# Ranks behind the scores, lists cleared in larger pieces, and another order of loads and stores in a fused attention and two-layer expert kernel

## Chip, cores and metric

One NeuronCore of a Trainium2 chip. The metric is device microseconds of the whole program on that core; 707.65 us is the median of three runs of the kernel before.

## What is computed

The reference runs a linear attention with a decaying state over 4 batches, 8 heads, 768 steps and head width 48, and feeds its output through two expert layers (8 experts, 3072 tokens, width 384, inner width 1024):

```python
for t in range(S):
    state = f[:, :, t, :, None] * state + einsum('bhd,bhe->bhde', k[:, :, t], v[:, :, t])
    y[:, :, t] = einsum('bhd,bhde->bhe', q[:, :, t], state)
x = y as (3072, 384)
# each layer: every token goes to the expert with the largest logit
expert = argmax(x @ w_gate, axis=1); gate = softmax(x @ w_gate)[expert]
out[i] = gate[i] * (relu(x[i] @ w1[expert[i]]) @ w2[expert[i]])   # f = sigmoid(f_logit)
```

The first layer keeps only the first `capacity` tokens of an expert; a token's place is its rank among the tokens of its expert.

## The kernel before

The attention works on 24 tiles of 128 tokens (`NTILE`), six per batch. `_attention` (L303) is one software pipeline: in step `it` every stage of the table `STAGES` (L217) runs in the order of the table on tile `it - lag`; the first six steps use the same table with `gates` later. All engines' programs are written in that order, so the table is the order of each engine's queue. The loop runs over 28 steps, and a tail (L620 on) with its own hand-written order finishes the last tiles and starts the first expert group.

Per tile and with their lags: `load_x` (0) loads F (the gate logits) and the two halves of X (keys and queries, transposed), `load_v` (4) loads V, all from SyncE, each into rotating buffers (3 F, 4 X, 4 V); `bound` (1, VectorE, DVE) clips F; `gates` (2, ScalarE, ACT); `sums` (3, TensorE, PE) makes the running sums G; `expand` (3, ACT); `factors` (3, DVE) makes KQ; `keys_t` (5, PE and a copy on ACT) transposes the keys; `scores` (5, PE); `masked` (5, DVE) reads the scores out of PSUM; `updates` and `states` (6) advance the state; `output_s`, `output_i` (7, PE) and `rows` (7, ACT) give the tile's rows; `rows_t`, `rows_c` (8) and `logits` (9) the router's logits. PSUM is shared: kp, G, xp and the warm-up spins rotate through the two buffers of tag "tr"; the scores `sc` and the updates `kv` have the one buffer of tag "sc".

Routing goes by groups of three tiles (`RG`). `g_copy`, `g_turn` and `g_choose` (10) put six small DVE operations (`st.choice`, L96 to L126, the last the one-hot `oha`; with it ACT's exponential `exa`) into the list `small`; `step()` calls strewn through `masked`, `factors`, `states` and `bound` issue them one by one. `g_rank` (11) flushes what is left and calls `place` (L128), five small PE matmuls that read the one-hots; `g_store` (11) lists the following operations, which turn ranks into slots. `g_list` (14, GpSimd) scatters token numbers into the list `tab1` in DRAM, `g_save` (14, SyncE) stores the group's rows (582 KB) to DRAM. In the table `g_rank` and `g_store` stand after `keys_t` and ahead of `sums`; `g_save` stands first. `lead` (12) runs once, for tile 11: a matmul and some DVE operations that mark the tokens of the first expert group.

`side(i)` (L1586) runs ahead of a step's stages: the two lists `tab1` and `tab2` in DRAM (491,520 bytes each) are cleared in steps 11 and 18 by `_clear` (L284) from an SBUF tile `env.fill` of 60 words per partition, and weight chunks (`raw`, 256 KB each) are fetched in some steps. `after(i)` splits weight chunks in the steps of `SPLITS` (L210): ACT copies, GpSimd subtracts.

The clear, as it is (n is 60, t is 16):

```python
    n = env.fill.shape[1]
    t = E * RC * TW // P // n
    eng.dma_start(out=tab.rearrange("(p t n) o -> p t (n o)", p=P, t=t), in_=env.fill.unsqueeze(1).to_broadcast([P, t, n]))
```

Of the kernel before, what the change touches and what calls it, by code (L numbers as in the profile page):

```python
# [9 lines left out]
F32 = mybir.dt.float32  # L10
F32R = mybir.dt.float32r
BF16 = mybir.dt.bfloat16
I32 = mybir.dt.int32
# [9 lines left out]
DM = H * D  # L23
E = 8
EP = 32
FF = 1024
P = 128
# [5 lines left out]
W = DM + 4  # L33
C_GATE = DM
C_TID = DM + 1
RC = 3840

TW = 4
BIG = 1048576.0
FIRST = 65536.0  # L40
FILL = 1 << 20
# [157 lines left out]
def _route(*args, **kw):  # L199
# [15 lines left out]


STAGES = (  # L217
    ("g_save", 14),
    ("load_v", 4),
    ("load_x", 0),  # L220
    ("g_copy", 10),
    ("gates", 2),
# [3 lines left out]
    ("bound", 1),  # L226
    ("warm", 0),
    ("keys_t", 5),
    ("g_rank", 11),
    ("g_store", 11),  # L230
    ("sums", 3),
    ("g_turn", 10),
    ("g_choose", 10),
# [1 line left out]
    ("expand", 3),  # L235
    ("output_i", 7),
    ("scores", 5),
    ("lead", 12),
    ("masked", 5),
    ("factors", 3),  # L240
    ("rows", 7),
    ("rows_c", 8),
    ("g_list", 14),
    ("logits", 9),
)

# [34 lines left out]
    tc.add_to_no_dep_group(key, ins)  # L281


def _clear(eng, env, tab):  # L284
    n = env.fill.shape[1]
    t = E * RC * TW // P // n
    eng.dma_start(
        out=tab.rearrange("(p t n) o -> p t (n o)", p=P, t=t), in_=env.fill.unsqueeze(1).to_broadcast([P, t, n])
    )


# [11 lines left out]
def _attention(tc, env, fn, kq, vn, x1, tab1, early, masks, first, side, after, first_group):  # L303


    nc = tc.nc
    with ExitStack() as ctx:
# [14 lines left out]
        pair = lambda t: t.rearrange("p (a e) -> p a e", a=NPAIR)  # L322
        tiles = {}
        grp = {}
        NVB = 4
        NXB = 4
        fbuf = [e1.tile([P, DM], F32, name=f"F{i}") for i in range(3)]
        xbuf = [e1.tile([P, 2, NPAIR, P], F32, name=f"X{i}") for i in range(NXB)]

        lbuf = [e1.tile([P, H, 64], F32, name=f"L{i}") for i in range(2)]  # L330
# [5 lines left out]
        for xb in xbuf[1:]:  # L336
            nc.gpsimd.memset(xb, 0.0)

        def load_x(i):
            t = tiles[i] = _Bag()  # L340
            t.F = fbuf[i % 3]
            t.X = xbuf[i % NXB]
            nc.sync.dma_start(out=t.F, in_=fn[i])
            if i < 2:
                masks(i)
            for h in range(2):
                nc.sync.dma_start(out=t.X[h * 64 : h * 64 + D], in_=kq[i, h])
# [211 lines left out]
        def flush():  # L559
            while small:  # L560
                step()
# [10 lines left out]
        def g_store(i):  # L572
            if i % RG == RG - 1:
                ro = tiles[i].ro
                for a, b in zip(ro.slots, ro.sums):
                    small.extend((a, b))
                small.extend(ro.sums[len(ro.slots) :])
# [27 lines left out]
        def spin(i, n):  # L605
# [3 lines left out]

        locals_ = {  # L610
            f.__name__: f
            for f in (load_x, load_v, bound, gates, sums, expand, factors, keys_t, scores, masked, updates, states,
                      output_s, output_i, rows, rows_t, rows_c, logits, g_copy, g_turn, g_choose, g_rank, g_store, g_save, g_list, warm, lead)
        }
        begin, turn, divide, product, parts = first_group(p_2, p_1)
        for it in range(NTILE + 4):
            side(it)
            for nm, lag in (STAGES if it >= NFIRST else FIRST_STAGES):
                if 0 <= it - lag < NTILE:
                    locals_[nm](it - lag)  # L620
                elif nm == "sums" and it - lag == NTILE:

                    spin(it, 1)
            after(it)
# [6 lines left out]
        updates(n - 1)  # L631
        states(n - 1)
        keys_t(n)
        flush()
        tiles[n - 6].ro.place()
        g_store(n - 6)
        rows_t(n - 3)
        rows_c(n - 3)
        output_i(n - 2)
        scores(n)  # L640
        masked(n)
        rows(n - 2)
        logits(n - 4)
# [62 lines left out]
def _attention_general(tc, env, f, k, q, v, x1, tab1):  # L706

    nc = tc.nc
    EG = 4
    EW = D // EG  # L710
    with ExitStack() as ctx:
        gp = ctx.enter_context(tc.tile_pool(name="g_in", bufs=1))
        gps = ctx.enter_context(tc.tile_pool(name="g_ps", bufs=1, space=PSUM))
        st = gp.tile([P, EW, D], F32, name="g_st")
        nc.vector.memset(st, 0.0)
        tm = gp.tile([P, EW, D], F32, name="g_tm")
        with tc.For_i(0, S, TSTEP) as t0:
            tl = {}
            for nm, src in (("f", f), ("k", k), ("q", q)):
                t = gp.tile([P, TSTEP, D], F32, name="g_" + nm, tag="g_" + nm)  # L720
                sv = src.rearrange("b h s d -> (b h) s d")[:, bass.ds(t0, TSTEP), :]
                for g in range(EG):
                    nc.sync.dma_start(out=t[g * 32 : (g + 1) * 32], in_=sv)
                tl[nm] = t
            vt = gp.tile([P, TSTEP, EW], F32, name="g_v", tag="g_v")
            for g in range(EG):
                sv = v.rearrange("b h s d -> (b h) s d")[:, bass.ds(t0, TSTEP), g * EW : (g + 1) * EW]
                nc.sync.dma_start(out=vt[g * 32 : (g + 1) * 32], in_=sv)
            ft = tl["f"]
            nc.scalar.activation(ft, ft, AF.Exp, scale=-1.0)  # L730
            nc.vector.tensor_scalar(out=ft, in0=ft, scalar1=1.0, scalar2=None, op0=ALU.add)
            nc.vector.reciprocal(out=ft, in_=ft)
            yt = gp.tile([P, TSTEP, EW], F32, name="g_y", tag="g_y")
            sh = [P, EW, D]
            for t in range(TSTEP):
                ob = lambda a: a[:, t : t + 1, :].to_broadcast(sh)
                nc.vector.tensor_tensor(out=st, in0=st, in1=ob(ft), op=ALU.mult)
                nc.vector.tensor_tensor(
                    out=tm, in0=ob(tl["k"]), in1=vt[:, t, :].unsqueeze(2).to_broadcast(sh), op=ALU.mult
                )  # L740
                nc.vector.tensor_tensor(out=st, in0=st, in1=tm, op=ALU.add)
                nc.vector.tensor_tensor(out=tm, in0=st, in1=ob(tl["q"]), op=ALU.mult)
                nc.vector.tensor_reduce(out=yt[:, t, :], in_=tm, axis=AX.X, op=ALU.add)
            for g in range(EG):
                for b in range(B):
                    dst = x1.rearrange("(b s) w -> b s w", b=B)[b, bass.ds(t0, TSTEP), 0:DM]
                    dst = dst.rearrange("s (h e) -> h s e", h=H)[:, :, g * EW : (g + 1) * EW]
                    nc.sync.dma_start(out=dst, in_=yt[g * 32 + b * H : g * 32 + (b + 1) * H])
        nc.vector.memset(env.cum1, 0.0)
        _clear(nc.gpsimd, env, tab1)  # L750
        tid = gp.tile([P, TW], I32, name="g_tid")
        nc.gpsimd.iota(tid, pattern=[[0, TW]], base=0, channel_multiplier=1)
        with tc.For_i(0, NT, P) as r0:
            xr = gp.tile([P, W], F32, name="g_xr", tag="g_xr")
            nc.sync.dma_start(out=xr[:, 0:DM], in_=x1[bass.ds(r0, P), 0:DM])
            nc.vector.memset(xr[:, DM:W], 0.0)
            xp = gps.tile([P, NCC, P], F32, name="g_xp", tag="g_xp")
            for cc in range(NCC):
                nc.tensor.transpose(xp[:, cc], xr[:, cc * P : (cc + 1) * P], env.ident)
            xT = gp.tile([P, NCC, P], F32, name="g_xT", tag="g_xT")  # L760
            nc.vector.tensor_copy(out=xT, in_=xp)
            rt = gps.tile([P, 64], F32, name="g_rt", tag="g_rt")
            for cc in range(NCC):
                nc.tensor.matmul(rt[:, 0:E], xT[:, cc], env.wg1[:, cc, 0:E], start=(cc == 0), stop=(cc == NCC - 1))
            su = _route(
                nc, env, rt[:, 32 : 32 + E].unsqueeze(1), rt[:, 0:E].unsqueeze(1), 1, P, env.cum1,
                xr[:, C_GATE : C_GATE + 1], "ag", lim=env.lim,
            )
            nc.sync.dma_start(out=x1[bass.ds(r0, P), DM:W], in_=xr[:, DM:W])
            _scatter1(tc, "tab1g", tab1, su, tid, E * RC - 1)  # L770
            nc.vector.tensor_scalar(out=tid, in0=tid, scalar1=float(P), scalar2=None, op0=ALU.add)
# [699 lines left out]
def tile_attention_moe_moe(  # L1471
# [5 lines left out]
    nc = tc.nc  # L1477
# [84 lines left out]
    with ExitStack() as mo:  # L1562
# [9 lines left out]
            tc.tile_pool(name=nm, bufs=b, side="right", reuse_waits="tile")  # L1572
        )
        env.xr = R("xr", 2, mo)
        early = ExitStack()
        sel0 = cs[:, C_SEL : C_SEL + E]

# [8 lines left out]
        def side(i):  # L1586
            if i == 5:
                load_small()
            if i == 11:
                _clear(nc.sync, env, tab1)  # L1590
            if i == 18:
                _clear(nc.sync, env, tab2)
            if i == 8:
                late_setup()
            if i in (7, 12, 16, 20, 21, 22):

                wts.ahead = (7, 12, 16, 20, 21, 22).index(i) + 1
                wts.fetch()
            if i == SNAP + 14:
                M.take(g0)  # L1600
            if i == SNAP + 15:
                M.index(g0)
            if i == NTILE + 4:
                for j in range(g0.J):
                    M.gather(g0, j)
# [52 lines left out]
    with tc.If(fl > 0), ExitStack() as mo:  # L1658
# [19 lines left out]
        with tc.If(rd > 0):  # L1678
# [3 lines left out]
                nc.vector.tensor_copy(out=env.caps, in_=env.capn.to_broadcast([P, E]))  # L1682
                _attention_general(tc, env, f_nat, k_nat, q_nat, v_nat, x1, tab1)
            nc.vector.memset(env.cum2, 0.0)
            _clear(nc.gpsimd, env, tab2)
            for i in range(NTILE):
                nc.sync.dma_start(out=out[i * P : (i + 1) * P, :], in_=env.zrow[:, 0:DM])
            tb = yrp.tile([P, 2, NOVF], I32, name="o_tb")
# [97 lines left out]
```

## Time and profile before

| what | value |
|---|---|
| three runs | 705.44, 707.65, 709.28 us (median 707.65) |
| the profiled execution | 706.58 us, its span 704.8 us, mean granted clock 0.975 |
| PE busy | 663.6 us of the span (94%) |
| DVE, ACT, GpSimd busy | 400.8, 305.6, 211.9 us |
| DMA | 97.55 MB, mean 138 GB/s over the span |

Times inside the execution are microseconds from the span's start. PE is TensorE's matmuls; the clock column is the share of full speed (2.4 GHz) that TensorE was granted. A wait "<- issue" is idle time for which the profile shows no releaser. The queue q8 of the DMA views carries instructions, q1 SyncE's transfers and q0 GpSimd's.

### The profile page before, as it was taken

The numbers are of one execution on the slowest core, as the hardware profiler recorded it, in microseconds if no ns is written. First come the engines' busy times: TensorE is split into PE (matmuls) and PEld (weight loads), VectorE is DVE, ScalarE is ACT, GpSimd is POOL, SyncE is SP. The second block draws the span as 40 slices with busy tenths as digits, with TensorE's granted clock in tenths as the row PEclk, the third lists the DMA queues.
The fourth block names the chain that finished last, engine by engine and source line by source line (L and its number), as shares of the span: only waits on it lengthen the run. The fifth ranks groups of instructions, "written<-read, shape, count | busy, mean of one in ns | idle before, by whom it ended". The sixth has DMA issues, their size and how long they took to land.

```text
span 704.8 us, 17652 instructions
## 1 busy us (share of the span) xinstructions
PE 663.6 (94%) x6867; PEld 615.6 (87%) x6867; DVE 400.8 (57%) x1067; ACT 305.6 (43%) x649; POOL 211.9 (30%) x232
## 2 busy tenths in 40 slices
PE   7889878888899999999999999999999999999995
PEld 4778767776799999999999999899998899999994
DVE  3644546554557657576566864557555455565642
ACT  4665546453345344344434443144334343354421
POOL 2122435246334114140422221234424132224211
PEclk9998999899999999999999999999999999999998
DMA  8885797412269344373737350177445354435300
GB/s 199 221 176 159 186 191 193 130 41 89 72 196 275 114 142 142 113 189 86 216 88 174 90 188 13 34 221 216 111 129 167 103 165 131 141 119 166 108 25 21
DMA packets 59439, 97.55 MB, mean 138 GB/s; under 512 B 15820, under 2 KB 29102, under 8 KB 59347
## 3 DMA queue, kind: packets, MB, share of 16 engines
q1 hardware_dynamic: 51667, 80.70, 41.7%
q0 software_dynamic: 7680, 15.64, 8.1%
q8 instruction: 56, 0.92, 0.6%
q14 instruction: 36, 0.29, 0.1%
HBM read 80.54 MB, written 16.60 MB: 138 GB/s over the span
## 4 chain that ended last, share of the span: by engine, by line
PE 86%; DMA 6%; DVE 3%; issue 3%; ACT 1%; POOL 0%; DVEq 0%; ACTq 0%; POOLq 0%
PE hpm L1142 29%; PE ypm L1166 10%; PE ypm L1168 10%; PE ypm L1167 10%; DMA out_dram<-yr,tdm 6%; PE G L374 4%; PE y L486 4%; PE tpm L1118 2%; PE sc L414 2%; PE y L476 2%; PE kv L439 2%; PE warm L608 2%; PE kp L403 2%; PE tym L904 2%; PE xp L510 1%
## 5 line engine op out<-in xcount | busy, mean ns | idle before, releaser
L1166 PE MATMUL ypm<-hhm,w1h 128*128 128x288 f32 (+11 forms) x456 | 153.6, 337 | 1.8 <-DVE hlm L1154 1.8
L1167 PE MATMUL ypm<-hlm,w1h 128*128 128x288 f32 (+11 forms) x456 | 150.1, 329 | 0.0
L1168 PE MATMUL ypm<-hhm,w1l 128*128 128x288 f32 (+11 forms) x456 | 150.1, 329 | 0.0
L1142 PE MATMUL hpm<-xhm,w0h 128*128 128x288 f32 (+11 forms) x432 | 147.2, 342 | 0.0
L1142 PE MATMUL hpm<-xhm,w0l 128*128 128x288 f32 (+11 forms) x432 | 143.0, 332 | 0.0
L1153 ACT ACTIVATE hhm<-hpm 128x288 fp32r<-128x288 f32 (+11 forms) x144 | 69.5, 483 | 168.1 <-PE hpm L1142 165.8
L1142 PE MATMUL hpm<-xlm,w0h 128*128 128x288 f32 (+11 forms) x432 | 137.5, 332 | 0.0
L1154 DVE SCALAR_TENSOR_TENSOR hlm<-hpm,hhm 128x288 fp32r<-128x288 f32 (+11 forms) x144 | 78.1, 542 | 101.5 <-ACT hhm L1153 101.3
L293 POOL DMA_INDIRECT xrm<-x,idcm x64 | 71.0, 1109 | 136.9 <-PE hpm L1142 57.3
L1166 PEld LDWEIGHTS ypm<-hhm,w1h 128*128 128x128 f32 x456 | 85.7, 188 | 4.3 <-DVE hlm L1154 1.9
L1168 PEld LDWEIGHTS ypm<-hhm,w1l 128*128 128x128 f32 x456 | 85.7, 188 | 2.0
L1167 PEld LDWEIGHTS ypm<-hlm,w1h 128*128 128x128 f32 x456 | 85.8, 188 | 1.7
L1142 PEld LDWEIGHTS hpm<-xhm,w0h 128*128 128x128 f32 x432 | 81.2, 188 | 2.2
L1142 PEld LDWEIGHTS hpm<-xhm,w0l 128*128 128x128 f32 x432 | 81.3, 188 | 1.7
L1142 PEld LDWEIGHTS hpm<-xlm,w0h 128*128 128x128 f32 x432 | 80.3, 188 | 1.9
L271 POOL DMA_INDIRECT tab<-pos,sum x30 | 33.5, 1118 | 141.4 <-DVE sum L181 135.0
L271 POOL DMA_INDIRECT out_dram<-yr,tdm x34 | 41.2, 1212 | 89.4 <-DVE yr L980 83.3
L1004 DVE TENSOR_TENSOR w0l<-raw,w0h 128x512 fp32r<-128x512 f32 x90 | 60.2, 686 | 9.3 <-ACT w0h L1003 8.9
L1004 DVE TENSOR_TENSOR w1l<-raw,w1h 128x512 fp32r<-128x512 f32 x90 | 59.7, 688 | 0.3
L1003 ACT CAST w0h<-raw 128x512 fp32r<-128x512 f32 x96 | 57.3, 617 | 1.0 <-DMA raw<-in_w_dram 1.0
L1003 ACT CAST w1h<-raw 128x512 fp32r<-128x512 f32 x96 | 56.9, 622 | 0.4 <-DMA raw<-in_w_dram 0.4
L421 DVE TENSOR_TENSOR SC<-sc,cs 128x512 f32<-128x512 f32 x24 | 16.6, 690 | 65.4 <-PE sc L414 65.4
(224 smaller groups left out, 914.6 us busy)
## 6 DMA issues: line engine op xcount, KB each, us to landing
raw<-in_w_dram SPq DMA_DIRECT2D x192, 256.0 KB
X<-in_kq_dram SPq DMA_DIRECT2D x48, 192.0 KB
x<-xr SPq DMA_DIRECT2D x8, 582.0 KB
F<-in_fn_dram SPq DMA_DIRECT2D x24, 192.0 KB
Vn<-in_vn_dram SPq DMA_DIRECT2D x24, 192.0 KB
xrm<-x,idcm POOLq DMA_INDIRECT x64, 4.6
tab<-fill SPq DMA_DIRECT2D x2, 480.0 KB
x<-yr SPq DMA_DIRECT2D x2, 388.0 KB
```

The lines of the kernel that those rows point to most:

```text
L271: ins = tc.nc.gpsimd.indirect_dma_start(out=dst, out_offset=bass.IndirectOffsetOnAxis(ap=idx, axis=0), in_=src, in_offset=None, bounds_che ...
L293: nc.gpsimd.indirect_dma_start(out=dst, out_offset=None, in_=src, in_offset=bass.IndirectOffsetOnAxis(ap=idx, axis=0), bounds_check=bound, ...
L374: nc.tensor.matmul(t.G[:, a], t.L[:, 2 * a : 2 * a + 2].rearrange("p h d -> p (h d)"), env.cs[:, C_INC : C_INC + P], start=True, stop=True,)
L486: nc.tensor.matmul(t.y[u, h, e], t.SC[u, h, a], t.Vn[u, v0 : v0 + D], start=False, stop=a == NPAIR - 1,)
L1003: nc.scalar.copy(out=hi, in_=raw)
L1004: eng.tensor_tensor(out=lo, in0=raw, in1=hi.bitcast(F32), op=ALU.subtract)
L1142: nc.tensor.matmul(hp[:, :N], w[:, c, fs], x[:, c, :N], start=(k == 0), stop=(k == len(parts) - 1))
L1153: nc.scalar.activation(hh[:, :N], hp[:, :N], AF.Relu)
L1154: nc.vector.scalar_tensor_tensor(out=hl[:, :N], in0=hp[:, :N], scalar=0.0, in1=hh[:, :N].bitcast(F32), op0=ALU.max, op1=ALU.subtract)
L1166: nc.tensor.matmul(g.yp[d][:, :N], w2h[:, fc, ds_], hh[:, :N], start=(fc == 0), stop=False)
L1167: nc.tensor.matmul(g.yp[d][:, :N], w2h[:, fc, ds_], hl[:, :N], start=False, stop=False)
L1168: nc.tensor.matmul(g.yp[d][:, :N], w2l[:, fc, ds_], hh[:, :N], start=False, stop=(fc == NFC - 1))
```

## The change

The table of stages: `load_f` is split from `load_x` and runs one step ahead (lag -1, four F buffers), `load_v` has lag 3 and five V buffers, and both stand first; `g_save` goes to the end of the table with lag 15; `g_rank` and `g_store` move behind `scores` and `lead`, and `lead` gets lag 13. In the tail the rank of the third-last group (tiles 15 to 17) goes behind `scores(n)`, and one spin stands where it was. The clears read a tile of 960 words per partition, one piece of 3840 bytes for each partition; it lies in a buffer of the pool of gathered rows and is filled by GpSimd at the start.

```diff
--- before.py
+++ after.py
@@ -215,8 +215,8 @@
 
 
 STAGES = (
-    ("g_save", 14),
-    ("load_v", 4),
+    ("load_f", -1),
+    ("load_v", 3),
     ("load_x", 0),
     ("g_copy", 10),
     ("gates", 2),
@@ -226,8 +226,6 @@
     ("bound", 1),
     ("warm", 0),
     ("keys_t", 5),
-    ("g_rank", 11),
-    ("g_store", 11),
     ("sums", 3),
     ("g_turn", 10),
     ("g_choose", 10),
@@ -235,12 +233,15 @@
     ("expand", 3),
     ("output_i", 7),
     ("scores", 5),
-    ("lead", 12),
+    ("lead", 13),
+    ("g_rank", 11),
+    ("g_store", 11),
     ("masked", 5),
     ("factors", 3),
     ("rows", 7),
     ("rows_c", 8),
     ("g_list", 14),
+    ("g_save", 15),
     ("logits", 9),
 )
 
@@ -281,11 +282,11 @@
     tc.add_to_no_dep_group(key, ins)
 
 
-def _clear(eng, env, tab):
-    n = env.fill.shape[1]
+def _clear(eng, fill, tab):
+    n = fill.shape[1]
     t = E * RC * TW // P // n
     eng.dma_start(
-        out=tab.rearrange("(p t n) o -> p t (n o)", p=P, t=t), in_=env.fill.unsqueeze(1).to_broadcast([P, t, n])
+        out=tab.rearrange("(p t n) o -> p t (n o)", p=P, t=t), in_=fill.unsqueeze(1).to_broadcast([P, t, n])
     )
 
 
@@ -322,9 +323,9 @@
         pair = lambda t: t.rearrange("p (a e) -> p a e", a=NPAIR)
         tiles = {}
         grp = {}
-        NVB = 4
+        NVB = 5
         NXB = 4
-        fbuf = [e1.tile([P, DM], F32, name=f"F{i}") for i in range(3)]
+        fbuf = [e1.tile([P, DM], F32, name=f"F{i}") for i in range(4)]
         xbuf = [e1.tile([P, 2, NPAIR, P], F32, name=f"X{i}") for i in range(NXB)]
 
         lbuf = [e1.tile([P, H, 64], F32, name=f"L{i}") for i in range(2)]
@@ -336,11 +337,14 @@
         for xb in xbuf[1:]:
             nc.gpsimd.memset(xb, 0.0)
 
+        def load_f(i):
+            t = tiles[i] = _Bag()
+            t.F = fbuf[i % 4]
+            nc.sync.dma_start(out=t.F, in_=fn[i])
+
         def load_x(i):
-            t = tiles[i] = _Bag()
-            t.F = fbuf[i % 3]
+            t = tiles[i]
             t.X = xbuf[i % NXB]
-            nc.sync.dma_start(out=t.F, in_=fn[i])
             if i < 2:
                 masks(i)
             for h in range(2):
@@ -609,10 +613,11 @@
...
         begin, turn, divide, product, parts = first_group(p_2, p_1)
+        load_f(0)
         for it in range(NTILE + 4):
...
@@ -631,13 +636,14 @@
         updates(n - 1)
         states(n - 1)
         keys_t(n)
-        flush()
-        tiles[n - 6].ro.place()
-        g_store(n - 6)
+        spin(n, 1)
         rows_t(n - 3)
         rows_c(n - 3)
         output_i(n - 2)
         scores(n)
+        flush()
+        tiles[n - 6].ro.place()
+        g_store(n - 6)
         masked(n)
         rows(n - 2)
         logits(n - 4)
...
@@ -1572,6 +1578,10 @@
             tc.tile_pool(name=nm, bufs=b, side="right", reuse_waits="tile")
         )
         env.xr = R("xr", 2, mo)
+
+        fill = env.xr.tile([P, 4, W], F32, name="xfill", tag="xr").rearrange("p j w -> p (j w)")
+        fill = fill.bitcast(I32)[:, 0 : E * RC * TW // P]
+        nc.gpsimd.memset(fill, FILL)
         early = ExitStack()
         sel0 = cs[:, C_SEL : C_SEL + E]
 
@@ -1587,9 +1597,9 @@
             if i == 5:
                 load_small()
             if i == 11:
-                _clear(nc.sync, env, tab1)
+                _clear(nc.sync, fill, tab1)
             if i == 18:
-                _clear(nc.sync, env, tab2)
+                _clear(nc.sync, fill, tab2)
             if i == 8:
                 late_setup()
             if i in (7, 12, 16, 20, 21, 22):
...
```

## Rows read from the trace of the kernel before

**Rows 1.** Page, the chain that ended last, share of the span by engine.

```profile
PE 86%; DMA 6%; DVE 3%; issue 3%; ACT 1%; POOL 0%; DVEq 0%; ACTq 0%; POOLq 0%
```

**Rows 2.** Windows by stage: length, busy us of each engine, clock, DMA share.

```profile
25.60:158.50 132.90, 112.73 (x2961) 99.95 (x2960) 70.67 (x196) 76.17 (x157) 45.30 (x68) 0.91 0.65 157
158.50:179.10 20.60, 16.27 (x410) 13.29 (x407) 9.91 (x47) 7.24 (x17) 11.68 (x13) 0.92 0.36 106
179.10:704.80 525.70, 514.66 (x3264) 489.73 (x3264) 308.30 (x805) 209.69 (x453) 149.68 (x134) 1.00 0.45 131
```

**Rows 3.** Timeline of PE: start, us, line (two sums; the last spin).

```profile
30.27 1.06 PE L374 MATMUL G<-cs,L 128*128 128x128 f32 x8
...
40.00 1.06 PE L374 MATMUL G<-cs,L 128*128 128x128 f32 x8
...
158.49 0.38 PE L608 MATMUL warm<-zrow,oneb 128*128 128x512 bf16 x1
```

**Rows 4.** Timeline of PE: a turn, breaks, rank waits (idle before, releaser).

```profile
43.43 0.46 PE L414 MATMUL sc<-KQ 64*64 64x64 f32 x16 [0.73 <-issue]
...
50.16 0.57 PE L414 MATMUL sc<-KQ 64*64 64x64 f32 x22 [1.67 <-issue]
...
73.84 0.41 PE L264 MATMUL rt<-cs,lts 96*128 96x96 f32 x3
...
80.94 0.17 PE L130 MATMUL rt<-oha,trib 128*128 128x24 bf16 x1 [2.57 <-DVE oha L120]
...
98.43 0.61 PE L486 MATMUL y<-Vn,SC 64*64 64x48 f32 x15 [3.37 <-issue]
...
109.43 0.55 PE L439 MATMUL kv<-Vn,KT 64*64 64x48 f32 x20 [0.61 <-issue]
...
138.43 0.68 PE L439 MATMUL kv<-Vn,KT 64*64 64x48 f32 x32 [3.23 <-issue]
...
166.38 0.17 PE L130 MATMUL rt<-oha,trib 128*128 128x24 bf16 x1 [3.19 <-DVE oha L120]
```

**Rows 5.** Waits of PE to 179.1 us: us in total, times, the longest.

```profile
PE rt L130 <- DVE oha L120: 13.3, 6, 3.2
```

**Rows 6.** DMA, all queues, from 90.4 to 94.9 us.

```profile
DMA packets 2020, 0.76 MB, mean 169 GB/s; under 512 B 1877, under 2 KB 1880, under 8 KB 2020
```

**Rows 7.** DMA, instruction queue, from 94.9 to 97 us: packets, MB, share.

```profile
q8 instruction: 1, 0.02, 5.1%
```

**Rows 8.** Windows of 10 us: busy by engine, granted clock, DMA share, GB/s.

```profile
80.00:90.00 10.00, 9.06 (x184) 8.19 (x186) 3.88 (x15) 4.77 (x10) 0.97 (x4) 0.83 0.69 180
120.00:130.00 10.00, 7.43 (x118) 6.38 (x118) 4.05 (x12) 3.96 (x9) 2.48 (x4) 0.66 0.67 181
```

**Rows 9.** Timeline of all engines around the rank of step 16.

```profile
76.35 0.69 DVE L421 TENSOR_TENSOR SC<-sc,cs 128x512 f32<-128x512 f32 x1 [2.15 <-PE sc L414]
...
77.71 0.66 PE L403 MATMUL kp<-cs,KQ 128*128 128x128 f32 x4
...
78.44 1.04 DVE L108 TENSOR_TENSOR dla<-lsa,mxa 128x24 f32<-128x24 f32 x1
...
79.64 0.57 ACT L405 COPY KT<-kp 128x512 f32<-128x512 f32 x1
```

**Rows 10.** Timeline of ACT in the tail: the copy of the last keys.

```profile
163.28 0.58 ACT L405 COPY KT<-kp 128x512 f32<-128x512 f32 x1 [1.32 <-PE kp L403]
```

**Rows 11.** DMA, all queues, from 76.5 to 82.4 us.

```profile
DMA packets 990, 1.55 MB, mean 262 GB/s; under 512 B 135, under 2 KB 699, under 8 KB 989
```

**Rows 12.** DMA, instruction queue, from 82.4 to 84 us.

```profile
q8 instruction: 1, 0.02, 4.0%
```

**Rows 13.** Timeline of PE: the first updates.

```profile
18.79 0.68 PE L439 MATMUL kv<-Vn,KT 64*64 64x48 f32 x32 [1.60 <-ACT L L365]
```

**Rows 14.** Timeline of GpSimd at the start: the X buffers cleared.

```profile
1.66 2.73 POOL L337 MEMSET X<- 128x1024 f32 x3
```

**Rows 15.** DMA, instruction queue, from 25.6 to 158.5 us.

```profile
q8 instruction: 24, 0.39, 1.3%
```

More of the change, by code (lines that the diff above doesn't have):

```diff
@@ L611, in _attention @@
             f.__name__: f
-            for f in (load_x, load_v, bound, gates, sums, expand, factors, keys_t, scores, masked, updates, states,
+            for f in (load_f, load_x, load_v, bound, gates, sums, expand, factors, keys_t, scores, masked, updates, states,
                       output_s, output_i, rows, rows_t, rows_c, logits, g_copy, g_turn, g_choose, g_rank, g_store, g_save, g_list, warm, lead)
@@ L749, in _attention_general @@
         nc.vector.memset(env.cum1, 0.0)
-        _clear(nc.gpsimd, env, tab1)
+        _clear(nc.gpsimd, env.fill, tab1)
         tid = gp.tile([P, TW], I32, name="g_tid")
@@ L1684, in tile_attention_moe_moe @@
             nc.vector.memset(env.cum2, 0.0)
-            _clear(nc.gpsimd, env, tab2)
+            _clear(nc.gpsimd, env.fill, tab2)
             for i in range(NTILE):
```

## The prediction

> **What bounds the kernel now.** I read the chain of waits first: 86% of it is TensorE (PE) [rows 1], so what moves the end is time in which PE stands or runs slowly. The windows by stage say where that is [rows 2]: the experts, from 179.1 us on, keep PE busy for 514.66 of 525.70 us at full clock, and no part of the change touches them. The attention loop from 25.6 to 158.5 us has PE busy for 112.73 of 132.90 us at a granted clock of 0.91. The whole case lies there and in its tail, to 179.1 us.
>
> How far is the loop from its own pace? Two undisturbed steps (a step is one tile) run from 30.27 to 40.00 us, 4.87 us each [rows 3]. From the sums at 40.00 to the spin that stands in for them at 158.49 are 17 steps: 118.5 us. At pace that would be 17 x 4.87 = 82.8 us, plus five turns of at most 0.41 us and five ranks of some 0.3 us (five matmuls of about 0.17 us, pipelined) [rows 4]: 86 us. **Some 32 us are lost.** The waits of PE and its timeline name them:
> - 13.3 us in six waits of the rank matmul (L130) for the one-hot on VectorE (DVE) [rows 5]; one is the 2.57 us at 80.94, the last the tail's 3.19 us at 166.38 [rows 4].
> - Four breaks of 0.73, 1.67, 3.37 and 0.61 us in the middle of a group of matmuls that waits for no operand [rows 4]. No instruction packet moves on the DMA engines from 90.4 to 94.9 us, one does right after [rows 6, 7], and PE, which stopped at 95.06, resumes at 98.43: I read these as PE's instruction fetch arriving late.
> - 3.23 us before the state updates at 138.43 [rows 4]: `updates` and `scores` share one PSUM tag, so it waits until `masked` has read the scores, and `lead`'s DVE operations stand ahead of `masked`.
> - Half clock (1.2 of 2.4 GHz): (1 - 0.91) x 132.9 = 12.0 us in the loop and (1 - 0.92) x 20.6 = 1.6 in the tail [rows 2]. A stretch of 10 us at 0.83 costs 1.7 us, one at 0.66 costs 3.4 [rows 8]. The 0.66 and three of about 0.83 follow rank waits (8.5 us), about 3.5 follow the breaks of 1.67 and 3.37, and the tail's follows its rank.
>
> **A. Ranks behind the scores.** The five small matmuls move; they issue no DMA, and DVE's order stays, since no DVE operation stands between the old place and the new. Around step 16 the DVE chain is masked at 76.35, then `dla` at 78.44, and the one-hot that lets the rank go at 80.94, 4.6 us after masked; PE had finished transposing the keys by 78.37 [rows 9, 4]. PE now first does sums, row transposes, outputs and scores, and reaches the new place 4.87 us after the last scores, which is 4.87 less 0.2 us after masked began: it just fits. In the four other loop ranks the chain takes 3.7 to 4.6 us. **The wait that comes next** is on ScalarE (ACT): its exponential for the rank waits for `dla`, which took 1.04 us beside GpSimd's weight split, and the copy of the transposed keys queues behind it, 79.64 to 80.21 [rows 9]. The row transposes take the PSUM buffer that this copy frees, and PE would be there after the sums, at 78.2 + 0.9 = 79.1: a new wait of 1.1 us. The same rows around the other four give 0.25, 0, 1.1 and 0. In the tail the key copy ends at 163.86 [rows 10] and the one-hot at 166.38; with a spin, transposes, outputs and scores in between (2.2 us) some 1.1 of the 3.19 us stay. Behind the rank PE has logits and the next step's outputs; behind its result DVE has the slots, in the order of before. A = -13.3 + 3.5 = **-9.8 us** (to -13.3 if DVE is quicker without GpSimd beside it; 0 if another wait takes all of it).
>
> **B. The clock after ranks.** 8.5 + 1.6 = 10.1 us are to be had. Clock fell after breaks of 1.67 us and more, not after 0.73, nor directly after the 3.23. New waits are 1.1 us or less, but `lead`'s stays and others may come. I take two thirds: **-6.5 us** (0 to -10.1).
>
> **C. Clears in 3840-byte pieces.** Each list of 480 KB goes out in 2048 pieces of 240 bytes now, after it in 128. From 90.4 to 94.9 us, 1877 of 2020 packets are under 512 bytes, and 0.76 MB move at 169 GB/s [rows 6]: at that rate of packets a clear needs nearly 5 us. At the 262 GB/s of a crowded stretch without a clear [rows 11] 480 KB need 1.9 us. So each gives back some 3 us of all 16 DMA engines. No fetch moved in the 4.5 us before 94.9, and PE ran out at 95.06; with 3 us less in the queue it does not. C = -(3.37 + 1.67) - 3.5 of clock = **-8.5 us** (0 to -8.5). What the page says against it: the Trainium skill, DMA: Bandwidth & Descriptors, Queues, rings and completion order, has each DMA engine serve its queues in turn, packet by packet, so that a fetch on its own queue would not wait behind another queue's backlog. By that C would be nil. Rows 6 and 7 speak for a wait behind the backlog but don't prove it; it is rival 2.
>
> **D. The cover that goes.** The rank waits have hidden late fetches too. Around step 16 none begins from 76.5 to 82.4 us, with a store, two X loads, V and F moving, and one does from 82.4 to 84 [rows 11, 12]; PE lost nothing because it stood for 2.57 us and then ran at half clock. Without that it would come to the end of its instructions some 3 us early. Step 22 repeats it. A store (582 KB a group) is issued one to two steps later and behind F, V and X, so it meets other fetches; of the loop's stores two fall among loads. I put **+5 us** (0 to +15, three breaks like that at 98.43 with 1.7 us of clock each).
>
> **E. Loads.** SyncE blocks on the same waits: F on the last step's gates, V on its outputs, X on its factors; each load queued behind them has a step or more before its use, and the store waits for gates long done. V a step earlier, with a fifth buffer, can shorten the 1.60 us before the first updates at 18.79 [rows 13], where V is queued behind four X; X queues behind one more F. **-1 us** (-2 to +1). GpSimd's added clear of 960 words costs about 0.9 us, by the 2.73 us of three X buffers of 1024 [rows 14]; it delays buffers that SyncE reaches later than that, so nothing, or 0.9 us if they are what is late.
>
> **F. `lead` one step later** flushes six choice operations ahead of itself, while PE is in outputs and scores; its own wait of 3.23 us moves along: 0 (-1 to +2).
>
> Sum: -9.8 - 6.5 - 8.5 + 5 - 1 = -20.8. The profiled execution took 706.58 us, within the runs' 705.44 to 709.28 and 1.07 under their median, so **686 us**.
>
> **Rivals.**
> 1. Fetches take the ranks' place. Loads, stores and weights must now pass in about 5 instead of 7 us a step, and the share of the DMA engines, 0.65 over the loop [rows 2], comes to 0.65 x 132.9 / 112 = 0.77. For it: the long fetch delay of step 16. Against: the regular steps of rows 3 had no break. D is then +15 and B half: 706.6 - 9.8 - 3 - 8.5 + 15 - 1 = 699 us.
> 2. The breaks are not the clears' work. For it: breaks of 0.73 and 0.61 us without a clear in the queue. C = 0, the rest as forecast: 694 us. Beside it stands the Trainium skill, Runtime: NRT & Kernel Launch, Instruction fetch mechanics: crossing an instruction block costs little and is mostly hidden.
> 3. Slower. Fetches come late at nearly every one of the loop's 24 blocks [rows 15], each break as at 98.43 (3.37 us and 1.7 of clock). From five such breaks on, 25 us, the gain of A, B, C and E (25.8) is eaten; eight give 706.6 - 25.8 + 8 x 5 = 721 us. Against: only four of the 24 are late now.
> 4. The order is changed but nothing is gained, since the key copy and the shared PSUM tag hold PE as long as the one-hot did: A and B nil, and D eats most of C: 703 to 707 us.
>
> **How the numbers follow.** Forecast 0.60, rival 1 0.18, rival 2 0.14, rival 3 0.04, rival 4 0.04. The range goes from all terms at their favourable ends (-13.3 - 10.1 - 8.5 - 1, about 674) to rival 1: 674 to 700. A measurement of this kernel tells some 0.5%, 3.5 us, from no change. Faster takes the forecast and rivals 1 and 2: 0.92; same rival 4: 0.04; slower rival 3: 0.04.
>
> **What would show it.** Right: rank matmuls without a DVE wait in the loop; row transposes that wait for ACT by about 1 us in two steps; no packets of 240 bytes and no break after the clears; a mean clock above 0.95 in the loop; sums starting every 4.9 to 5.2 us; experts unchanged at about 526 us. Wrong: new "issue" breaks behind stores or X loads, with the fetch late; the 3.37 us break still there at the second clear; a shift at the experts.

## The result, and the profile after

Four runs of the changed kernel took 688.11 to 691.49 us, median 689.44, against 707.81 for the kernel before in the same comparison: a ratio of 0.9746 with a 95% interval of 0.9709 to 0.9783. The forecast was 686 us with a range of 674 to 700 and 0.92 for faster. The profiled execution took 689.96 us, with a span of 688.1, 16.7 us less than the one of before.

The page, chain by engine and all DMA packets (before, the packets of the span were 59,439, of them 15,820 under 512 bytes: the 4096 pieces of 240 bytes are what went):

```profile
PE 87%; DMA 7%; DVE 2%; issue 2%; ACT 1%; POOL 0%; DVEq 0%; ACTq 0%; POOLq 0%
...
DMA packets 55599, 97.55 MB, mean 142 GB/s; under 512 B 11724, under 2 KB 25006, under 8 KB 55507
```

Windows by stage of the changed kernel, cut at the same events as [rows 2]: the sums of the step that began at 25.6 there, the spin in place of the sums, the first expert matmul (length; busy us of PE, PEld, DVE, ACT, GpSimd; clock, DMA share, GB/s):

```profile
24.80:144.30 119.50, 106.49 (x2961) 94.42 (x2960) 70.80 (x196) 75.41 (x157) 45.01 (x68) 0.96 0.66 174
144.30:161.50 17.20, 15.37 (x411) 12.28 (x408) 9.86 (x46) 7.10 (x17) 11.72 (x13) 1.00 0.45 131
161.50:688.10 526.60, 515.58 (x3264) 489.79 (x3264) 308.29 (x805) 209.94 (x453) 151.42 (x134) 0.99 0.45 131
```

The loop gave 13.4 us, the tail 3.4, the start 0.8; the experts took 0.9 more. With the same 2961 matmuls in the loop, PE stood idle for 119.50 - 106.49 = 13.01 us instead of 20.17 (7.2 less), and was busy for 106.49 instead of 112.73 (6.2 less): the second is the clock. The waits of PE in the loop and most of the tail name most of the 13 us (further breaks without an operand follow one by one below):

```profile
PE kv L443 <- issue: 3.5, 2, 2.7
PE kv L443 <- DVE SC L425: 2.4, 1, 2.4
PE xp L514 <- ACT KT L409: 2.0, 2, 1.0
...
PE rt L259 <- DVE skip L1591: 1.4, 1, 1.4
...
PE rt L130 <- DVE oha L120: 0.2, 1, 0.2
```

Against 13.3 us in six waits [rows 5], the ranks (L130) wait 0.2. In their place stand two waits of the row transposes for the key copy on ACT, and breaks without an operand ("issue"). In PE's timeline (start, length, operation, idle time before it):

```profile
61.03 0.45 PE L443 MATMUL kv<-Vn,KT 64*64 64x48 f32 x17 [0.77 <-issue]
74.11 0.55 PE L514 MATMUL xp<-cs,xr 128*128 128x128 f32 x3 [1.00 <-ACT KT L409]
76.88 0.46 PE L418 MATMUL sc<-KQ 64*64 64x64 f32 x15 [0.86 <-issue]
87.11 0.61 PE L490 MATMUL y<-Vn,SC 64*64 64x48 f32 x15 [0.60 <-issue]
92.11 0.82 PE L378 MATMUL G<-cs,L 128*128 128x128 f32 x5 [1.14 <-issue]
98.98 0.88 PE L443 MATMUL kv<-Vn,KT 64*64 64x48 f32 x20 [2.69 <-issue]
113.55 0.55 PE L514 MATMUL xp<-cs,xr 128*128 128x128 f32 x3 [1.00 <-ACT KT L409]
127.30 0.42 PE L259 MATMUL rt<-xT,wg1s 128*32 128x128 f32 x6 [1.36 <-DVE skip L1591]
130.70 0.57 PE L443 MATMUL kv<-Vn,KT 64*64 64x48 f32 x12 [2.37 <-DVE SC L425]
```

With two of 0.36 and 0.30 us (at 42.63 and 52.45) the breaks sum to 6.7 us in the loop, against 6.4 in [rows 4]. They are others, though: the 1.67 and 3.37 behind the clears are gone, 0.86, 1.14 and 2.69 are new. They are read as late instruction fetches: at the longest PE stopped at 96.29 us; no packet of q8 moves from 90.7 to 96.4, and one fetch does from 96.4 to 97.6 (DMA, instruction queue, in that window):

```profile
q8 instruction: 1, 0.02, 5.7%
```

In all seven breaks of the loop PE resumes 1.3 to 1.5 us after such a fetch has landed.

The last two lines of the timeline are the step of `lead`, which had one wait of 3.23 us [rows 4]. Behind it the clock falls:

```profile
130.00:136.00 6.00, 5.30 (x63) 4.88 (x65) 2.49 (x5) 1.67 (x3) 0.74 (x3) 0.50 0.02 3
```

### The profile page after: what moved, and what is told of

Read it like the earlier page. It is cut to its first block, busy times and chain, and to the rows that moved or that the text cites. A ratio compares the mean times of both kernels' runs of the same rounds, so it can differ in the third digit from the quotient of the medians.

```text
span 688.1 us, 17651 instructions
## 1 busy us (share of the span) xinstructions
PE 657.0 (95%) x6866; PEld 609.1 (89%) x6868; DVE 401.8 (58%) x1067; ACT 305.0 (44%) x649; POOL 214.1 (31%) x233
## 4 chain that ended last, share of the span: by engine, by line
PE 87%; DMA 7%; DVE 2%; issue 2%; ACT 1%; POOL 0%; DVEq 0%; ACTq 0%; POOLq 0%
PE hpm L1148 30%; PE ypm L1172 10%; PE ypm L1173 10%; PE ypm L1174 10%; DMA out_dram<-yr,tdm 6%; PE y L490 3%; PE G L378 3%; PE tpm L1124 2%; PE kv L443 2%; PE kp L407 2%; PE y L480 2%; PE tym L910 2%; PE warm L612 2%; PE sc L418 1%; PE tym L985 1%
## 5 line engine op out<-in xcount | busy, mean ns | idle before, releaser
L1132 ACT CAST xhm<-tpm 128x336 fp32r<-128x336 f32 (+8 forms) x62 | 24.1, 433 | 66.3 <-PE tpm L1124 66.2
```

The lines of the kernel that those rows point to most:

```text
L1132: nc.scalar.copy(out=g.xh[:, :, s], in_=tp[:, :, :Pr])
```

## The experiments

The first four stood on one chip beside runs of the kernel before with a median of 709.28 us, the next four beside 717.81, the last four beside 718.84. On these last two chips every kernel that was traced (the kernel before was not) had a break of about 3.1 us in the tail that the first traces do not have, so kernels are compared by their ratio to the kernel before, and by the loop alone: from the sums at 24.77 us in the changed kernel (their like in each trace) to the spin. That is 132.88 us before and 119.52 after the change.

**The ranks alone.** `g_rank` and `g_store` behind `scores`, in the tail too; all else as before.

```diff
-    ("g_rank", 11),
-    ("g_store", 11),
...
     ("scores", 5),
     ("lead", 12),
+    ("g_rank", 11),
+    ("g_store", 11),
```

> Before, with the ranks alone moved behind the scores (tail and spin included; lead stays at lag 12). Forecast (A, B, D): no wait of the rank for the one-hot in the loop, two waits of the row transposes for the key copy of about 1.0 us, lead's wait 3 us with no logits waiting for it; the two breaks after the small-piece clears stay (1.7 and 3.4 us), and the fetch that the rank wait of step 16 covered now shows as a break of 1 to 3 us in step 16 or 17. Time 707.8 - 9.8 - 8 + 4 = 694, ratio 0.975 to 0.985. Rival 1 (fetches take the ranks' place): breaks in the loop sum to over 14 us, ratio above 0.985. Rival 4 (another wait takes all of it): ratio above 0.995.

Measured: 699.2 us, ratio 0.9868 (0.9796 to 0.9939). The six rank waits are gone; breaks and key-copy waits in PE's timeline are these:

```profile
51.62 0.64 PE L414 MATMUL sc<-KQ 64*64 64x64 f32 x22 [3.10 <-issue]
78.74 0.55 PE L510 MATMUL xp<-cs,xr 128*128 128x128 f32 x3 [1.00 <-ACT KT L405]
82.05 0.46 PE L414 MATMUL sc<-KQ 64*64 64x64 f32 x15 [1.40 <-issue]
...
106.29 0.64 PE L439 MATMUL kv<-Vn,KT 64*64 64x48 f32 x20 [1.87 <-issue]
120.98 0.55 PE L510 MATMUL xp<-cs,xr 128*128 128x128 f32 x3 [1.00 <-ACT KT L405]
124.41 0.90 PE L414 MATMUL sc<-KQ 64*64 64x64 f32 x18 [1.58 <-issue]
136.92 0.82 PE L439 MATMUL kv<-Vn,KT 64*64 64x48 f32 x32 [3.24 <-issue]
```

In the loop 10.1 us of rank waits went, 2.6 of key-copy waits came, and the breaks sum to 8.7 us with one of 0.72, where they were 6.4. Steps 16 and 22, where the forecast looked for a late fetch behind the rank wait that hid it, have breaks of 1.40 and 1.58 us. The one behind the first clear grew from 1.67 to 3.10; the 3.37 behind the second, which the forecast had staying, is gone, though the clear still goes out in small pieces. PE came to it through the break of 1.40 and a stretch at half clock; that this is why is not shown. The loop took 128.12 us, the tail 17.23 instead of 20.62. So the tail's gain is the ranks' alone, and in the loop about half of theirs is given back in this form.

Of the loop's clock nothing came back. PE is busy for as long as before (112.73 us) at the same granted clock:

```profile
26.55:154.67 128.12, 112.81 (x2960) 99.79 (x2959) 72.33 (x196) 75.63 (x157) 45.48 (x68) 0.91 0.70 162
```

Stretches of 6.8 us at half clock now begin in or just after the breaks of 1.40 and 1.58 us. The ratio lies above the forecast's 0.975 to 0.985 and just inside rival 1's, whose 14 us of breaks did not come.

**The clears alone.** The tile of 960 words and `_clear(nc.sync, fill, ...)`; ranks, loads and stores as before.

```diff
-                _clear(nc.sync, env, tab1)
+                _clear(nc.sync, fill, tab1)
...
-                _clear(nc.sync, env, tab2)
+                _clear(nc.sync, fill, tab2)
```

> Before, with the clears alone in pieces of 3840 bytes. Forecast (C): the breaks of 1.67 us near 48 and 3.37 us near 95 are gone or under 0.6 us each, and so is the half clock behind them; the rank waits stay at 13 us; 708 - 8.5 = 699, ratio 0.984 to 0.992. Rival 2 (the breaks are not the clears' work): both breaks stay, ratio 0.996 to 1.003.

Measured: 703.2 us, ratio 0.9918 (0.9882 to 0.9954). The two large breaks are gone, and with them the two stretches of 3.4 us at half clock behind them; near the first there is a break of 0.40:

```profile
53.88 0.55 PE L486 MATMUL y<-Vn,SC 64*64 64x48 f32 x12 [0.40 <-issue]
...
97.52 0.17 PE L130 MATMUL rt<-oha,trib 128*128 128x24 bf16 x1 [2.18 <-DVE oha L120]
103.98 0.55 PE L439 MATMUL kv<-Vn,KT 64*64 64x48 f32 x20 [1.88 <-issue]
133.13 0.68 PE L439 MATMUL kv<-Vn,KT 64*64 64x48 f32 x32 [3.23 <-issue]
```

Part of the gain fell to the next rank, whose wait after the second clear grew from 1.11 to 2.18 us, as PE came to it sooner, and breaks of 0.93 (at 30.08) and 1.88 are new. So the clears alone give 6.1 us of medians, where the forecast has 8.5; the ratio is at the edge of the forecast's 0.984 to 0.992.

**The clears as they were, in other steps.** Pieces of 240 bytes still, in steps 9 and 15 instead of 11 and 18.

```diff
-            if i == 11:
+            if i == 9:
                 _clear(nc.sync, env, tab1)
-            if i == 18:
+            if i == 15:
                 _clear(nc.sync, env, tab2)
```

> Before, with both clears still in 240-byte pieces but in steps 9 and 15 in place of 11 and 18. If a late instruction fetch behind the clear makes the breaks, they move with it: none over 0.8 us near 48 and near 95, and one of 1 us or more at about 38 us (one block after the clear of step 9); behind the clear of step 15 the rank wait of step 16 may hide part of it. Rival 2: breaks of 1.6 and 3.3 us stay near 48 and 95, and none is added.

A single execution: 703.56 us, which alone says nothing of the time. The breaks moved with the clears, to 40.86 and 79.07 us, and none is left near 50 or 95:

```profile
40.86 0.68 PE L476 MATMUL y<-S,KQ 64*64 64x48 f32 x32 [2.81 <-POOL w0l L1004]
...
79.07 0.73 PE L476 MATMUL y<-S,KQ 64*64 64x48 f32 x28 [2.82 <-issue]
82.44 0.18 PE L130 MATMUL rt<-oha,trib 128*128 128x24 bf16 x1 [0.64 <-DVE oha L120]
```

The releaser named at 40.86 is a GpSimd operation that PE does not read there; a fetch lands 1.7 us before PE resumes, as one lands 1.4 us before 79.07. Together with the run before this settles rival 2: the two large breaks were the clears' work, though fetches have a queue of their own. The next rank then waits 0.64 us only: a break and a rank wait cover the same lateness.

**The loads and stores alone.** F a step ahead, V at lag 3, store last at lag 15, one more buffer each; ranks, clears and `lead` as before.

```diff
-    ("g_save", 14),
-    ("load_v", 4),
+    ("load_f", -1),
+    ("load_v", 3),
...
+    ("g_save", 15),
```

> Before, with the order of loads and stores alone changed (F a step ahead, V a step earlier, the store last and a step later, the two extra buffers). Forecast (E): 0 to 2 us quicker, from the first updates, ratio 0.997 to 1.000; rank waits, and the breaks after the small-piece clears, stay. If instead the order of the store was what made the breaks, the one near 95 us goes and the ratio is 0.990 to 0.994.

Measured: 708.33 us, ratio 0.9981 (0.994 to 1.0021), no difference. The first clear's break is 2.26 us, the second's is 0.25, and the rank behind that waits 2.28 where it waited 1.11: moved, not gained.

```profile
101.74 0.17 PE L130 MATMUL rt<-oha,trib 128*128 128x24 bf16 x1 [2.28 <-DVE oha L120]
```

The product of the three parts' ratios is 0.977, and all of them together gave 0.9746: no large part hides in their combination.

**`lead` back at 12.** The trace after had shown a new wait of 1.36 us of the logits for `lead`'s copy, and half clock behind the step; this puts back the one number.

```diff
-    ("lead", 13),
+    ("lead", 12),
```

> The changed kernel with one number undone: `lead` at 12 again instead of 13, the step it had before. Theory (the term for `lead` was mis-sized: one step later its matmuls find the PSUM buffer of the last group's logits not yet copied out, and its wait and the one before the updates are followed by a stretch at half clock): no wait of `lead`'s matmul for the skip copy (1.36 us in the changed kernel), the one before the updates back near 3.2 us, no half clock behind it; ratio to the changed kernel about 0.995, so some 686 us, and 0.969 to the kernel before. Rival a (the place of `lead` doesn't matter, any place costs 7 us with its clock): 689 us, 0.974. Rival b (earlier, its DVE work now stands ahead of a step-22 rank whose wait the change removed): a new wait of the last ranks of 1 to 3 us and 688 to 690 us.

Measured: 700.34 us, ratio 0.9764 (0.9726 to 0.9803). The logits' wait went, but nothing was gained. In PE's timeline of those steps (two of the three small breaks, and the idle time before the updates):

```profile
122.59 0.34 PE L480 MATMUL y<-S,KQ 64*64 64x48 f32 x6 [0.42 <-issue]
123.36 0.48 PE L480 MATMUL y<-S,KQ 64*64 64x48 f32 x15 [0.43 <-issue]
125.63 0.76 PE L443 MATMUL kv<-Vn,KT 64*64 64x48 f32 x32 [1.79 <-issue]
```

and behind it:

```profile
127.00:129.00 2.00, 2.00 (x12) 2.00 (x11) 0.95 (x3) 0.59 (x1) 0.51 (x1) 0.50 0.00 0
```

Breaks of 0.31, 0.42 and 0.43 and idle time of 1.79 us stand where 3.73 stood, with 3.4 us at half clock behind them. By the time the theory falls: rival a, that either place costs the same, holds.

**The exponential behind the one-hot.** On the kernel just shown, so that ACT's copy of the keys has nothing ahead of it that waits for `dla`.

```diff
-        st.ex = tl("ex", [E])
-        nc.scalar.activation(st.ex, st.dl, AF.Exp)
...
+        st.ex = tl("ex", [E])
+        nc.scalar.activation(st.ex, st.dl, AF.Exp)
```

> As lead_12, and the exponential for the rank moves behind the one-hot into `place`, so that the copy of the transposed keys on ScalarE has nothing that waits for `dla` ahead of it. Theory (the row transposes of steps 16 and 22 wait 1.00 us each because that exponential holds the key copy): both waits gone, 2.0 us less than lead_12, ratio to it 0.997, some 684 us. Rival a (the key copy is late for another reason): both waits stay, same time as lead_12. Rival b (the wait gone, PE comes 1 us earlier to the rank, whose one-hot then is late): rank waits of about 1 us in steps 16 and 22 in place of them, same time.

Measured: 702.35 us, ratio 0.9807 (0.9767 to 0.9847). Both key-copy waits (0.90 and 0.27 us in the kernel just shown) are gone, as the theory said of them, and the time with them is not: two matmul groups after the place of the first, PE now breaks off by itself.

```profile
74.54 0.46 PE L418 MATMUL sc<-KQ 64*64 64x64 f32 x15 [1.33 <-issue]
```

`lead` at 12 alone had 0.90 us of key-copy wait there and no break above 0.4. It looks like the same exchange as with the ranks, a wait of 1 us that covered a late fetch of 1 us, though one trace of each does not prove it.

**Ranks and clears without the loads.** Loads, stores, buffers and `lead` as before the change.

```diff
-    ("load_f", -1),
-    ("load_v", 3),
+    ("g_save", 14),
+    ("load_v", 4),
...
-    ("g_save", 15),
```

> The kernel before with the ranks moved and the clears in larger pieces, and nothing else: loads, stores, buffers and `lead` as before. Terms A, B, C and D without E: the forecast has E at -1 us, so 1 us above lead_12, ratio to the kernel before 0.970. Rival a (the order of the loads is what keeps the fetches on time once the ranks hide them no longer): more breaks than lead_12, over 2 us each behind the stores or X loads, and 692 to 697 us. Rival b (the new order is what makes the late fetches, by F, raw and X in one burst): fewer breaks than lead_12, no break of 2.69 us near step 19, and 682 to 685 us.

Measured: 703.02 us, ratio 0.9797 (0.9739 to 0.9855); the loop took 125.05 us.

```profile
80.93 0.46 PE L414 MATMUL sc<-KQ 64*64 64x64 f32 x15 [3.23 <-issue]
...
108.71 0.54 PE L476 MATMUL y<-S,KQ 64*64 64x48 f32 x10 [2.33 <-issue]
```

Step 16 has the full 3 us that the forecast had put there; in the traces with the new order of loads it is at most 1.43. The profile thus speaks for rival a: the order of the loads, worth nothing alone, holds fetches back less once the ranks hide none. By the ratios, 0.9797 against 0.9743 to 0.9764, it is some 0.4%, which the intervals do not tell from nothing.

**The store early again.** The changed kernel with `g_save` at 14, first in the table.

```diff
+    ("g_save", 14),
     ("load_f", -1),
...
-    ("g_save", 15),
```

> The changed kernel with the store put back: `g_save` at 14, first in the table, ahead of the loads, `lead` at 13 as changed. If the place of the store sets which fetch is late (term D), breaks behind it change by 2 us or more: those of the changed kernel at 0.77, 0.86, 1.14 and 2.69 us move or go, and the time differs from the changed kernel by over 0.4%. If the late fetches come from the loads (F, raw, X in a burst), the break of 2.69 us near step 19 stays and the time is the same within 0.3%.

Measured: 704.53 us, ratio 0.9801 (0.9746 to 0.9856), loop 121.31 us. The break near 99 is gone and others are there, the sum of those above 0.4 us being about the same:

```profile
77.33 0.70 PE L418 MATMUL sc<-KQ 64*64 64x64 f32 x15 [1.42 <-issue]
104.34 0.56 PE L480 MATMUL y<-S,KQ 64*64 64x48 f32 x10 [1.78 <-issue]
```

That fits a store that sets which fetch is late, but does not show it: with `lead` behind `masked` (below) the break near 99 is gone too, and there the store has not moved. Whether its old place costs time the intervals leave open.

**The changed kernel again**, unedited, on the chip of the three runs that follow.

> The changed kernel itself, once more, to stand beside the others on one chip. Ratio to the kernel before 0.975, as measured (0.971 to 0.978). In the trace the wait of `lead`'s matmul for the skip copy (1.36 us), the one of 2.37 us before the updates and half clock behind it again; the late fetch of 2.69 us near step 19 again, if it is the kernel's and not the execution's.

Measured: 700.47 us, ratio 0.9743 (0.9688 to 0.9798). The ratio repeats to 0.0003. The single executions do not: six of them lie between 696.1 and 705.7, and the breaks differ from those of the first trace.

```profile
101.79 0.64 PE L443 MATMUL kv<-Vn,KT 64*64 64x48 f32 x20 [1.32 <-issue]
130.63 0.42 PE L259 MATMUL rt<-xT,wg1s 128*32 128x128 f32 x6 [0.61 <-DVE skip L1591]
134.04 1.10 PE L443 MATMUL kv<-Vn,KT 64*64 64x48 f32 x32 [2.38 <-DVE SC L425]
165.85 0.55 PE L514 MATMUL xp<-cs,xr 128*128 128x128 f32 x3 [3.08 <-issue]
```

The 2.69 us near 99 are 1.32 here, at the same place in the program: the size is the execution's. The wait of `lead`'s matmul is 0.61 for 1.36, and the key-copy waits are 0.26 each for 1.00. The wait of 2.38 before the updates is the same, and 6.9 us at half clock go with it. The loop took 122.87 us, with PE busy for 109.88, 3.4 us more than in the first trace.

**`lead` behind `masked`**, at lag 12, so that its DVE operations no longer stand ahead of the one that reads the scores out.

```diff
-    ("lead", 13),
...
     ("masked", 5),
+    ("lead", 12),
```

> The changed kernel with `lead` at 12 and behind `masked` in the table, so that its DVE operations stand behind the one that reads the scores out. Theory (the updates wait because `lead`'s DVE chain stands ahead of `masked`, and the clock falls behind that wait; the place of `lead` by one step is not what counts): no wait over 0.5 us before those updates, no logits wait, no half clock there: 3.7 of waits and 3.4 of clock, so 4 to 7 us under the changed kernel, 0.990 to 0.994 of it, about 0.967 of the kernel before. Rival a (another late fetch or wait takes its place in those two steps): a break of 1.5 to 3 us there, same time as the changed kernel. Rival b (the DVE chain of `lead` now delays the factors and with them the keys): a wait of keys or scores of 1 us or more one or two steps later, 2 to 4 us gained.

Measured: 699.1 us, ratio 0.9753 (0.9707 to 0.9798), the same as the changed kernel. The wait before the updates is gone; `lead`'s own matmul waits instead, for the count that the last rank's operations on DVE write:

```profile
122.91 0.17 PE L1590 MATMUL rt<-cum,oneb 128*128 128x8 bf16 x1 [1.29 <-DVE cum L155]
```

From 127 to 129 us the clock is at 0.50 here too (the stretch is 3.4 us). So the theory's wait went and its gain did not come, as rival a has it. One step later and behind `masked` was not tried.

**A weight chunk a step earlier**, on the changed kernel, and **both of the last two**.

```diff
-            if i in (7, 12, 16, 20, 21, 22):
+            if i in (7, 12, 16, 19, 21, 22):
...
-                wts.ahead = (7, 12, 16, 20, 21, 22).index(i) + 1
+                wts.ahead = (7, 12, 16, 19, 21, 22).index(i) + 1
```

> The changed kernel with the fetch of a weight chunk moved from step 20 to step 19, so that two chunks of 256 KB no longer follow each other in SyncE's queue (at 91.28 us in the changed kernel). Theory (the late fetch near 99 us, 2.69 us, lies behind that burst of X, two chunks, F and V): the break gone or under 1 us, and the half clock of 1.7 us behind it; up to 4 us less, ratio to the changed kernel 0.994 to 0.997. Rival (the fetch is late for what runs in any case, X and the chunk after it, or the burst moves a step ahead to the clear of the second list): a break of 2 to 3 us there or one step earlier, same time within 0.3%.

> Both of the last two edits. If each takes away a loss of its own, the gains add: 6 to 10 us under the changed kernel, 0.986 to 0.991 of it, about 0.963 of the kernel before. If a late fetch comes in wherever PE runs faster, the sum is that of the better of the two alone, or less.

Measured: 701.04 us, ratio 0.976 (0.9718 to 0.9801), for the chunk alone; 697.6 us, 0.970 (0.9654 to 0.9746), for both. The break in question is 1.05 us with the chunk moved, 1.32 with both:

```profile
98.20 0.55 PE L443 MATMUL kv<-Vn,KT 64*64 64x48 f32 x20 [1.05 <-issue]
```

As the unedited kernel on that chip had 1.32 as well, this says nothing of the burst as the cause. Both edits together have the lowest median and the shortest loop, 117.10 us, but in that trace the tail took 28.19 us where the unedited kernel's took 23.56. The median is 0.996 of the changed kernel's, where 0.986 to 0.991 was forecast, and the intervals overlap, so no version is shown to beat it.

## Why the prediction was right, and where it was off

The direction, the place and the size were right: the time lies in the range, 3.4 us above the forecast, and the gain is in the loop and its tail. That it came so close is in part luck: B came out 2.2 us better and D 2.1 us worse than forecast, and these cancel. Term by term, for the two profiled executions, 706.58 and 689.96 us:

| term | forecast | measured | from |
|---|---|---|---|
| A ranks | -9.8 | -10.6 | loop -10.1 of rank waits, +2.0 of key-copy waits; tail's idle time -2.5 |
| B clock after ranks | -6.5 | -8.7 | PE busy -6.2 in the loop and -0.9 in the tail, less the clock in C, D and F; what is left over, in no run by itself |
| C clears | -8.5 | -8.5 | breaks of 1.67 and 3.37 gone; clock 3.5 as forecast (the clears alone took away 3.4) |
| D cover that goes | +5 | +7.1 | other breaks 1.3 before, 6.7 now; half clock behind the one at 98.98, 1.7 |
| E loads | -1 | -0.8 | the start; the loop starts at 23.1 to 25.1 us in the traces with the new order, at 25.1 to 26.6 with the old |
| F `lead` | 0 | +3.9 | waits 3.73 for 3.23; half clock for 6.8 us |
| experts | 0 | +0.9 | windows |

- **A** held in its mechanism and its details: the key copy that queues on ACT behind the exponential is late by 1.00 us in exactly the two steps named, where 1.1 was forecast (0.26 in the second trace of this kernel). Only the tail was better: its rank waits 0.17 us where 1.1 of the 3.19 were to stay.
- **B** came out, but not from the ranks alone. Granted clock over the loop is 0.96 and in the tail 1.00, against 0.91 and 0.92. With only the ranks moved the tail got its clock back and the loop none (112.81 us busy, before 112.73), as half clock followed breaks instead; with ranks and clears but the old loads PE was busy for 111.25 us in the loop, beside 107.25 with the new loads on the same chip (`lead` at 12 in both, one trace each). The 8.7 us are what one trace has left over, and the same kernel's second trace has 3.4 us less of them.
- **C** held, and the moved clears show its cause: breaks of 2.81 and 2.82 us followed the 240-byte pieces to their new steps. What a clear costs depends on when PE comes to it, as the second one in the run of the ranks alone cost no break. The Trainium skill, DMA: Bandwidth & Descriptors, section Queues, rings and completion order, has each DMA engine serve its queues in turn, packet by packet; by that rule, as the prediction read it, C would have been nil. The runs, with 5.0 us of breaks gone, don't agree with that; where the fetches were held up they don't show.
- **D** was right in kind, short by 2 us. Five breaks of 0.60 to 2.69 us are late fetches of the loop after the change; in step 16, where a rank wait had stood, it was 0.86 us in this order and 3.23 with the old loads. That waits had hidden the other four is argued, not shown. Rival 1 is this term at its upper bound; it did not come to that. The loop has 23 fetches, so most still cost nothing. The Trainium skill, Runtime: NRT & Kernel Launch, section Instruction fetch mechanics, calls the crossing of a block mostly hidden: that holds for their number, not for the 6.7 us that the others took.
- **F is the term that failed.** The step was "its own wait of 3.23 us moves along: 0". The wait did, at 3.73, but the sum rested on one execution in which no half clock followed it, here in a window of the kernel before:

```profile
139.00:142.00 3.00, 3.00 (x57) 2.79 (x52) 1.65 (x5) 1.67 (x3) 0.69 (x2) 1.00 0.03 8
```

In the four runs with one part changed, the moved clears among them, all with `lead` where it was, this wait is 3.22 to 3.24 us as before, and the clock behind it was at half for 3.4 us (1.7 us lost), as with the clears alone:

```profile
134.00:137.00 3.00, 3.00 (x17) 3.00 (x16) 1.35 (x5) 1.11 (x3) 0.51 (x1) 0.50 0.02 5
```

So the words "nor directly after the 3.23" read a habit out of one trace. The step that failed is the clock behind `lead`'s wait, put at nothing: it cost 1.7 us in those four runs and 3.4 in the changed kernel, where the stretch was twice as long, 6.8 us. That `lead` one step later is the cause was my first explanation, and it is not borne out: at 12, at 13 and behind `masked` the kernel takes the same time within the intervals, with another wait in that step each time. Why the stretch was longer is open. With `lead` at 13, waits of 0.6 and 2.4 us stand before 6.9 us at half clock in the second trace of the changed kernel, but before 3.4 us with the store early or the weight chunk moved, so the waits' size does not decide it.

Of the signs that the prediction named, one did not come: the sums start 5.35 us apart at the median of the loop's 20 steps, and only eight lie within 4.9 to 5.2 us. And new breaks with a late fetch, named as a sign of being wrong, came in part: they are D.

## What to carry to other kernels

A wait that is long and early hides whatever comes late behind it: when it is taken away, look in the same steps for instruction fetches and copies that were covered, and expect to give some of the gain back as breaks "<- issue". Write large fills in large pieces: here 2048 packets of 240 bytes held up an instruction fetch, and TensorE, which has nothing to do with the fill, stood for 3.37 us. And read what follows a wait (the clock above all) from several executions or several waits of its length before its cost is set at nothing.

## What was not expected

A small DVE operation beside a weight split on GpSimd can take ten times its time. In the changed kernel the 128x24 operation of the choice (L112) takes 0.18 us at its median, but beside a split 1.88, and an operation of `lead` on 128x8 takes 1.73 (timeline of DVE and GpSimd):

```profile
124.84 1.88 DVE L112 SCALAR_TENSOR_TENSOR t1a<-dla,cs 128x24 f32<-128x24 f32 x1
...
125.38 1.29 POOL L1010 TENSOR_TENSOR w1l<-raw,w1h 128x512 fp32r<-128x512 f32 x1
...
128.04 1.73 DVE L855 SCALAR_TENSOR_TENSOR cum<-cs,skip,cum 128x8 bf16<-128x8 f32 x1
...
128.46 1.27 POOL L1010 TENSOR_TENSOR w1l<-raw,w1h 128x512 fp32r<-128x512 f32 x1
```

Each ends just as the GpSimd operation does, within 0.06 us. These two operations, 3.6 us together, stand in the chain that holds the updates back at 130.70; moving the split out of this step was not tried.
